# Splitting the first chunk's features one block earlier, and a decode ring of two buffers behind it

## The chip, the cores and the metric

The kernel runs on one core of one Trainium2 chip. The metric is the time of one execution in device microseconds (us): 709.61 us before, the median of 3 runs (709.57 to 710.03). Lower is better.

## The reference

Three layers follow each other. First comes attention over a sliding window of 64 positions (4 sequences of 576 tokens, 8 heads of 64). Its 2304 tokens of width 512 then pass a dense feed-forward layer, and a mixture of 8 experts picks one expert per token.

```python
def _moe_ref(x, w_in, w_out):
    h = x @ w_in                      # 2304x512 @ 512x2048
    g = np.where(h >= 1, h, np.where(h <= -1, 0.0, (h + 1) ** 2 / 4))
    return g @ w_out                  # 2304x2048 @ 2048x512
def _moe2_ref(x, modality_id, w_gate, modality_bias, w1, w2):
    logits = x @ w_gate + modality_bias[modality_id]
    e_idx = np.argmax(logits, axis=1)
    ...
        h = np.maximum(x[mask] @ w1[e], 0.0)
        out[mask] = gate_w[mask, None] * (h @ w2[e])
```

The weights `w_in` and `w_out` arrive as 64-bit floating-point words, which the kernel turns into 32-bit floats itself.

## The kernel before

The dense layer works through 6 chunks of 384 tokens (`NC = 6`, `CT = 384`). Each chunk runs over 16 blocks of 128 features (`NF = 16`). For block f, `l1(c, f)` multiplies the chunk's tokens with w_in tile (0, f), the ScalarE (ACT) and VectorE (DVE) apply the activation (`relu` on ACT, `act2` on DVE), and two steps later `l2(c, f)` (`LAG = 2`) multiplies the result with w_out tile (1, f). A weight tile is called (kind, f), with kind 0 for w_in and 1 for w_out.

**Whole and split.** A 32-bit product can be made in two ways. Whole: the tile is used as it is; each matmul then appears in the trace as two instructions (L508 for `l1`, L575 for `l2`). Split: the operand is rounded to a high part by ACT (`split_hi`, L330, for weights; `gsplit_hi`, L561, for activations), DVE subtracts it to get a low part (`split_lo`, L335; `gsplit_lo`, L566), and three matmuls high-high, high-low, low-high stand for each product (L529 and L581). In chunk 0 the blocks below `FS` are whole and those from `FS` on are split. The chunk's tokens are split by `x0_hi` and `x0_lo` in the steps FS-3 and FS-2. Every later chunk uses split tiles alone, so all 32 weight tiles must be split by the time that chunk 1 needs them.

**Decode.** The 64-bit words come in 16 pairs of tiles. Pair p is loaded by SyncE (SP) with two DMAs of 512 KB (`dec_load`, L273), read by ACT (`dec_abs`, L284, from pair 11 on also L286), then clamped and merged by DVE (`dec_clamp`, L293; `dec_merge`, whose last line is L310 or L312). The words lie in a ring of three buffers, pair p in buffer p % 3. So the load of pair p + 3 can go when pair p is merged. Buffers 0 and 1 are halves of the tile `dec`; buffer 2 lies in the tags T30 and T31. `turn[f]` lists the pairs decoded in step f: pairs 7 and 8 in step 6, pair 9 in step 7, pair 10 in step 8, and then one in each step to pair 15 in step 13. `dec_abs` of a pair runs in the step ahead.

**Where split tiles live.** A split tile needs a buffer (a tag T0 to T31). `free` is the list of tags that can be had, first in, first out. A decoded pair gives its tag back when both its tiles have been split. `soon` lists the splits made during chunk 0. The rest, `later`, is split during chunk 1, at the start of each step: two tiles each, but one in steps 5 and 7.

**Feature blocks 10 to 15 of chunk 1** have their `l1` run ahead, in chunk 0's steps 10 to 15 (`FJ = 10`). Their activations wait in three tiles `kept` (tags T25, T28, T29, two blocks in each) and are split in chunk 1's steps 1 to 6. Their tags join `free` in steps 2, 4 and 6:

```python
        if c == 1 and 1 <= f <= NF - FJ:
            gsplit(1, FJ + f - 1)
            if f % 2 == 0:
                free.append(f"T{NF + (9, 12, 13)[f // 2 - 1]}")
```

The split activations `gh` and `gl` have two buffers each.

**Order.** In chunk 0 (`step0`) the order on TensorE (PE), DVE, ACT and GpSimd (POOL) is the order in which the code writes it. From chunk 1 on, a planner orders DVE, ACT and POOL; PE is again in written order from step 3 of chunk 1. There a step is: `gsplit`, attention for chunk 2, `split`, `l1(1, f)`, `l2(1, 8 + f)` for f below 8, `l2(1, f - 2)`. SP is in written order throughout.

Of the kernel before, what the change touches and what calls it, by code (L numbers as in the profile page):

```python
# [21 lines left out]
DM = H * D  # L22
KD = DM // P
FF = 2048
NF = FF // P
# [49 lines left out]
def moe_kernel(ctx, tc, qT, kT, v, w_in, w_out, mod, wg, wgT, mbias, w1, w2, cst, tri, empty, out, spec):  # L75
# [17 lines left out]
    def tile_of(shape, name, dt=F32, tag=None, bufs=1):  # L93
        pool = sb if (tag or name) in WIDE else sm
        return pool.tile(shape, dt, name=name, tag=tag or name, bufs=bufs)
# [48 lines left out]
    def load_v(i):  # L144
        n, w0 = window(i) if i else (P, 0)
        if i == 1:
            vs[i] = vs[0]
            return
        vs[i] = lend(2 + i // 2, i % 2) if i < BPC else tile_of([P, DM], f"v{i}", tag="v", bufs=2)
        SP.dma_start(vs[i][:n], v[w0 : w0 + n, :])  # L150
# [58 lines left out]

    PRE = 3  # L210
    LAG = 2
    FS, FJ = 9, 10
    TWICE = (6,)

    def part(kind, f, lo):
# [24 lines left out]
    NPR = len(pairs)  # L240
# [1 line left out]
    for f in range(FS, NF - 1):  # L242
        soon.setdefault(f + 1, []).append((1, f))
    soon[NF - 1].append((1, NF - 1))
    for f, kf in ((14, (0, 0)), (14, (0, 1)), (15, (0, 2)), (15, (1, 0))):
        soon[f].append(kf)
    turn, p = [], 1
    for f in range(NF + 1):
# [2 lines left out]
    later = [kf for kfs in pairs for kf in kfs if kf not in sum(soon.values(), [])]  # L251
    lone_kf = later[-1]
    dts = {}

    late = {}

    def raw(p, u):
        if p % 3 == 2:
            if (p, u) not in late:
                late[p, u] = tile_of([P, 2 * DM], f"dec{p}_{u}", I32, tag=f"T{2 * NF - 2 + u}")  # L260
            return late[p, u]
        o = (p % 3 * 2 + u) * 2 * DM
        return dec[:, o : o + 2 * DM]

    def words(p, u):
# [3 lines left out]
    def dec_load(p, us=(0, 1)):  # L269
        if p < NPR:  # L270
            for u in us:
                kind, f = pairs[p][u]
                SP.dma_start(raw(p, u), (w_out if kind else w_in)[f].bitcast(I32))  # L273

    def three(p):
        return p >= turn[FS][0]

    def dec_abs(p, us=(0, 1)):
        if p < NPR:
# [8 lines left out]
    def dec_clamp(p, us=(0, 1)):  # L288
        if p < NPR:
            t = dts[p]  # L290
            for u in us:
                tf = t[u].bitcast(F32)
                V.tensor_scalar(tf, tf, d0 if three(p) else c0, d1 if three(p) else c1, op0=ALU.max, op1=ALU.min)  # L293
            for u in us if not three(p) else ():
                V.tensor_scalar(t[u], t[u], 5, 2, op0=ALU.logical_shift_left, op1=ALU.logical_shift_right)
# [37 lines left out]
    def split_lo():  # L333
        kf, t, tag, w = halves.pop(0)
        V.tensor_tensor(t[:, WB:], w, t[:, :WB].bitcast(F32), op=ALU.subtract)  # L335
        parts[kf] = (t, tag)
        if kf != lone_kf:
            p = pair_of[kf]
            left[p] -= 1
            if not left[p]:  # L340
                free.append(f"T{p}")
# [94 lines left out]
    def att_sum(i):  # L436
        sm = at[i][1]
        V.tensor_scalar_add(sm, sm, 1e-9)
        V.reciprocal(sm, sm)  # L439
# [24 lines left out]
    def att_pv(i):  # L464
        o = 0
        if i < BPC:
            xo = ps.tile([P, KD, BLK], F32, name=f"xo{i}", tag="h", bufs=2)
        elif i < PAIRED:
            xo = aux([P, KD, BLK], f"xo{i}")
        else:  # L470
            o = i % GB
            xo = xos[i - 1] if o else aux([P, KD, GT], f"xo{i}")
        ts = at.pop(i)
        vt = vs.pop(i)
        w = window(i)[0]
        for hp in range(KD):
            for a in range(2):
                c = turned(i, a)
                T.matmul(
                    xo[a * D : (a + 1) * D, hp, o * BLK : (o + 1) * BLK],  # L480
                    vt[:w, (2 * hp + a) * D : (2 * hp + a + 1) * D],
                    ts[:w, hp, c * BLK : (c + 1) * BLK],
                    start=True,
                    stop=True,
                )
        xos[i] = xo

    def att_x(i):
        xo = xos.pop(i)
        c, n = divmod(i, BPC)  # L490
        dst = slice(n * BLK, (n + 1) * BLK)
        if i >= PAIRED:
            xos.pop(i + 1)
            dst = slice(n * BLK, n * BLK + GT)
        if c == 0:
            A.copy(whole_x[0][:, :, dst], xo)
            return
        xh, xl = xs[c]
        A.copy(xh[:, :, dst], xo)
        V.tensor_tensor(xl[:, :, dst], xo, xh[:, :, dst].bitcast(F32), op=ALU.subtract)  # L500
# [9 lines left out]
    def l1_tile(t):  # L510
        if t == 0:
            hs[0, 0] = ps.tile([P, CT], F32, tag="h", name="h0_0", bufs=2)
        l1_whole(0, slice(t * P, (t + 1) * P))
# [18 lines left out]
    def relu(c, f):  # L532
        h = hs[c, f]
        u = tile_of([P, CT], f"u{c}_{f}", tag="u", bufs=2)
        A.activation(u, h, AF.Relu, bias=half, scale=0.5)  # L535
        A.activation(u, u, AF.Square)  # L536
        us[c, f] = u

    def act2(c, f):
        u, h = us[c, f], hs.pop((c, f))  # L540
        g = u
        if c == 1 and f >= FJ:
            j, o = divmod(f - FJ, 2)
            if not o:
                kept.append(tile_of([P, 2 * WB], f"kept{j}", tag=f"T{NF + (9, 12, 13)[j]}"))
            g = us[c, f] = kept[j][:, o * CT : (o + 1) * CT]
        if c == 0 and f < FS:
            g = gs[c, f] = tile_of([P, CT], f"g{c}_{f}", tag="gh" if f % 2 else "gl", bufs=2)
        V.scalar_tensor_tensor(g, u, 1.0, h, op0=ALU.min, op1=ALU.max)  # L549
# [8 lines left out]
    def gsplit_hi(c, f, u):  # L558
        gh = tile_of([P, CT], f"gh{c}_{f}", F32R, tag="gh", bufs=2)
        gl = tile_of([P, CT], f"gl{c}_{f}", F32R, tag="gl", bufs=2)  # L560
        A.copy(gh, u)  # L561
        gs[c, f] = (gh, gl)

    def gsplit_lo(c, f, u):
        gh, gl = gs[c, f]
        V.tensor_tensor(gl, u, gh.bitcast(F32), op=ALU.subtract)  # L566
# [483 lines left out]
    dec_abs(1, (1,))  # L1050
    l1_tile(1)
    l1_tile(2)
    dec_load(3)

    S0 = {c: (1, 5, 9) for c in range(NC)}
    S0[1] = (0, 3, 6)
# [49 lines left out]
    def step0(f):  # L1106
        split0 = f - 1 >= FS
        join = f >= FJ
        at_step = {f - st: BPC + k for k, st in enumerate(FIRST)}
        if f == NF - 3:  # L1110
            free.extend(f"T{NF + k}" for k in (14, 15))
        if f >= 1:
            act2(0, f - 1)
            if split0:
                gsplit_hi(0, f - 1, us[0, f - 1])
        if f - 1 >= FJ:
            act2(1, f - 1)
        for kf in soon.get(f, []):
            split_lo()
        if split0:  # L1120
            gsplit_lo(0, f - 1, us[0, f - 1])
        dec_clamp(*turn[f][:1] or [NPR])
        if 3 in at_step:
            att_pv(at_step[3])
        if 1 in at_step:
            att_sum(at_step[1])
        if 3 in at_step:
            att_x(at_step[3])
        dec_merge(*turn[f][:1] or [NPR])
        for p in turn[f][1:]:  # L1130
            dec_clamp(p)
            dec_merge(p)
        l1(0, f)
        relu(0, f)
        if 1 in at_step:
            load_v(at_step[1])
        two = [at_step[0], at_step[0] + 1] if at_step.get(0, 1) % 2 == 0 else []
        if two:
            att_mm(*two)
            for i in two:  # L1140
                att_loads(i)
        for p in turn[f]:
            dec_load(p + 3)
        if 2 in at_step:
            att_tr(at_step[2])
        for p in turn[f + 1][:1]:
            dec_abs(p)
        if 1 in at_step:
            att_scale(at_step[1])
        if f in (FS - 3, FS - 2):  # L1150
            x0_hi(f - FS + 3)
        for i in two:
            att_max(i)
        if 0 in at_step:
            att_exp(at_step[0])
        if f in (FS - 3, FS - 2):
            x0_lo(f - FS + 3)
        if join:
            l1(1, f)
            relu(1, f)  # L1160
        if f >= LAG:
            l2(0, f - LAG)
        for p in turn[f + 1][1:]:
            dec_abs(p)
        for kf in soon.get(f + 1, []):
            split_hi(kf)
        if f == FS - 1:
            token_bias()
        if f == NF - 1:
            free.extend(f"T{NF + k}" for k in (10, 11))  # L1170
            hold_back(gs[0, f - 1][0].bitcast(F32))
            wgb.append(tile_of([P, E, DM], "wgb", tag="dec"))
            SP.dma_start(
                wgb[0].rearrange("p e d -> p (e d)"),
                wgT.rearrange("(o e) d -> o (e d)", o=1).broadcast_to([P, E * DM]),
            )
# [7 lines left out]
    for n in range(len(its) + LAG):  # L1184
        c, f = its[n] if n < len(its) else (NC, n - len(its))
# [4 lines left out]
        if c == 0:  # L1190
            step0(f)
            continue
# [145 lines left out]
```

## Time and profile before

| what | value |
|---|---|
| median of 3 runs | 709.61 us |
| the profiled execution's own time | 710.55 us |
| its span, first to last instruction | 708.7 us |
| PE, DVE, ACT busy | 697.2, 458.9, 383.3 us |
| mean granted clock of TensorE | 0.998 of full |

The profiled execution lasts 1.85 us longer than its span, and 0.94 us longer than the median. A time in a view counts from the first instruction. A matmul that is still draining counts as busy, so a short wait shows best in the starts of the instructions, which the timeline gives; L529 is line 529 of the kernel. In the timeline a row holds start, duration, engine, line, operation, out<-in and how many were joined; brackets give the idle time ahead and what ended it.

### The profile page before, as it was taken

The numbers are of one execution on the slowest core, as the hardware profiler recorded it, in microseconds if no ns is written. First come the engines' busy times: TensorE is split into PE (matmuls) and PEld (weight loads), VectorE is DVE, ScalarE is ACT, GpSimd is POOL, SyncE is SP. The second block draws the span as 40 slices with busy tenths as digits, with TensorE's granted clock in tenths as the row PEclk, the third lists the DMA queues.
The fourth block names the chain that finished last, engine by engine and source line by source line (L and its number), as shares of the span: only waits on it lengthen the run. The fifth ranks groups of instructions, "written<-read, shape, count | busy, mean of one in ns | idle before, by whom it ended". The sixth has DMA issues, their size and how long they took to land. (4 is left out here: it accounts for less than half of the span.)

```text
span 708.7 us, 13085 instructions
## 1 busy us (share of the span) xinstructions
PE 697.2 (98%) x4523; PEld 601.2 (85%) x4523; DVE 458.9 (65%) x1408; ACT 383.3 (54%) x930; POOL 129.2 (18%) x188
## 2 busy tenths in 40 slices
PE   8999999999999999999999999999999999999995
PEld 5655799888888888988888998899989999998984
DVE  5999997897497538862697648867665454534110
ACT  6799998656555536554555445545444553443120
POOL 3000201013001201120111502041037414111101
PEclk9999999999999999999999999999999999999999
DMA  8986614402221103220310015145555655446401
GB/s 304 312 298 238 215 36 172 133 8 63 75 81 48 41 13 98 61 68 16 98 46 31 2 45 179 63 88 185 174 118 165 224 178 178 164 150 207 148 6 48
DMA packets 48525, 84.59 MB, mean 119 GB/s; under 512 B 6928, under 2 KB 20880, under 8 KB 48320
## 3 DMA queue, kind: packets, MB, share of 16 engines
q1 hardware_dynamic: 44064, 73.64, 31.9%
q0 software_dynamic: 4240, 9.79, 4.7%
q8 instruction: 38, 0.62, 0.4%
q14 instruction: 39, 0.32, 0.1%
q10 hardware_dynamic: 144, 0.22, 0.1%
HBM read 74.17 MB, written 9.67 MB: 118 GB/s over the span
## 5 line engine op out<-in xcount | busy, mean ns | idle before, releaser
L529 PE MATMUL h<-xh,w 128*128 128x384 f32 x640 | 179.4, 341 | 0.0
L581 PE MATMUL py<-w,gh 128*128 128x512 f32 x522 | 162.0, 392 | 0.0
L529 PEld LDWEIGHTS h<-xh,w 128*128 128x128 f32 x640 | 117.0, 188 | 4.4 <-issue 1.4
L581 PEld LDWEIGHTS py<-w,gh 128*128 128x128 f32 x522 | 96.6, 188 | 16.0
L529 PE MATMUL h<-xl,w 128*128 128x384 f32 x320 | 107.4, 336 | 0.0
L581 PE MATMUL py<-w,gl 128*128 128x512 f32 x261 | 102.8, 397 | 0.9 <-DVE gl L566 0.9
L912 PE MATMUL hp<-zh,e 128*128 128x384 f32 x384 | 101.5, 337 | 0.0
L927 PE MATMUL yo<-e,hm 128*128 128x512 f32 x324 | 93.5, 395 | 0.0
L535 ACT ACTIVATE u<-h,half 128x384 f32<-128x384 f32 x96 | 55.4, 577 | 66.9 <-PE h L529 59.9
L838 DVE TENSOR_TENSOR e<-wr,e 128x512 fp32r<-128x512 f32 x96 | 64.0, 689 | 35.9 <-ACT e L837 33.9
L635 DVE CUSTOM_DVE_ANT_0 prod<-y,wgb 128x512 f32<-128x512 f32 x120 | 85.5, 713 | 1.4
L549 DVE SCALAR_TENSOR_TENSOR u<-u,h 128x384 f32<-128x384 f32 x81 | 44.6, 551 | 61.8 <-ACT u L536 61.6
L561 ACT CAST gh<-u 128x384 fp32r<-128x384 f32 x81 | 41.5, 512 | 64.3 <-DVE u L549 34.4
L912 PEld LDWEIGHTS hp<-zh,e 128*128 128x128 f32 x384 | 69.7, 188 | 1.2 <-DVE hm L915 0.3
L927 PEld LDWEIGHTS yo<-e,hm 128*128 128x128 f32 x324 | 59.6, 188 | 12.0 <-issue 0.6
L449 POOL TENSOR_TENSOR s<-s,sm 128x512 f32<-128x512 f32 (+1 forms) x24 | 27.5, 1149 | 214.7 <-DVE sm L439 71.8
L837 ACT CAST e<-wr 128x512 fp32r<-128x512 f32 x96 | 56.7, 616 | 16.6 <-DMA wr<-in_w 16.3
L912 PE MATMUL hp<-zl,e 128*128 128x384 f32 x192 | 64.3, 335 | 0.0
L529 PEld LDWEIGHTS h<-xl,w 128*128 128x128 f32 x320 | 60.1, 188 | 1.9
L566 DVE TENSOR_TENSOR gl<-u,gh 128x384 fp32r<-128x384 f32 x81 | 45.9, 567 | 24.4 <-ACT gh L561 23.5
L581 PEld LDWEIGHTS py<-w,gl 128*128 128x128 f32 x261 | 48.9, 188 | 11.9 <-DVE gl L566 1.5
L914 ACT ACTIVATE hm<-hp 128x384 fp32r<-128x384 f32 x48 | 23.6, 491 | 55.0 <-PE hp L912 54.9
(235 smaller groups left out, 1026.3 us busy)
## 6 DMA issues: line engine op xcount, KB each, us to landing
wr<-in_w SPq DMA_DIRECT2D x96, 256.0 KB, 3.1
dec<-in_w_in SPq DMA_DIRECT2D x16, 512.0 KB, 5.8
dec<-in_w_out SPq DMA_DIRECT2D x16, 512.0 KB, 4.2
v<-in_v SPq DMA_DIRECT2D x27, 256.0 KB, 3.2
k<-in_kT SPq DMA_DIRECT2D x15, 384.0 KB, 4.2
yd<-y SPq DMA_DIRECT2D x18, 256.0 KB, 2.4
q<-in_qT SPq DMA_DIRECT2D x32, 128.0 KB, 2.9
m<-in_w SPq DMA_DIRECT2D x16, 256.0 KB, 4.9
```

The costliest lines, as they stand in the source:

```text
L449: G.tensor_tensor(s, s, bc(sm, 2, window(i)[0]), op=ALU.mult)
L529: T.matmul(h, wi(f, a)[:, k, :], b, start=n == 0, stop=n == 3 * KD - 1)
L535: A.activation(u, h, AF.Relu, bias=half, scale=0.5)
L549: V.scalar_tensor_tensor(g, u, 1.0, h, op0=ALU.min, op1=ALU.max)
L561: A.copy(gh, u)
L566: V.tensor_tensor(gl, u, gh.bitcast(F32), op=ALU.subtract)
L581: T.matmul(ys[c][t], a[:, sl], wo(f, b), start=f == first and n == 0, stop=f == last and n == 2)
L635: V.tensor_tensor_reduce(prod, yt[t], wgb[0][:, e, :], 1.0, 0.0, ALU.mult, ALU.add, lg[:, t, e : e + 1])
L837: A.copy(wpart(i, p, 0), t)
L838: V.tensor_tensor(wpart(i, p, 1), t, wpart(i, p, 0).bitcast(F32), op=ALU.subtract)
L912: T.matmul(hp, w1s(i, f, k, a), b[:, k, :], start=n == 0, stop=n == 3 * KD - 1)
L927: T.matmul(yo, a[f][:, sl], w2s(i, f, b), start=n == 0, stop=n == 3 * NF2 - 1)
```

## The change

Chunk 0 uses split operands from block 8 on (`FS` 9 to 8), so the tiles (0, 8) and (1, 8) and the activation of block 8 are split in chunk 0, and the tokens are split one step earlier, in steps 5 and 6. Tiles (0, 2) and (1, 0) are no longer split at the end of chunk 0 and move to the front of `later`. The ring of three holds to pair 8 (`LAST3`); from pair 9 on there are two buffers, the halves of `dec`, so pair p + 2 is loaded when pair p is merged. T30 and T31 join `free` in step 7, not in step 13. Which pairs take the three-instruction form (`three`) stays as it was, from pair 11. The list `later` keeps 14 tiles:

- before: (0,3) (1,1) (1,2) (0,4) (1,3) (0,5) (1,4) (0,6) (1,5) (0,7) (1,6) (0,8) (1,7) (1,8)
- after: (0,2) (1,0) (0,3) (1,1) (1,2) (0,4) (1,3) (0,5) (1,4) (0,6) (1,5) (0,7) (1,6) (1,7)

```diff
-    FS, FJ = 9, 10
+    FS, FJ = 8, 10
...
-    for f, kf in ((14, (0, 0)), (14, (0, 1)), (15, (0, 2)), (15, (1, 0))):
+    for f, kf in ((14, (0, 0)), (14, (0, 1))):
         soon[f].append(kf)
...
+    LAST3 = turn[TWICE[0]][-1]
+    ring = [p % 3 if p <= LAST3 else (p - LAST3 - 1) % 2 for p in range(NPR)]
+    after = {}
+    for p in range(3, NPR):
+        after.setdefault(max(n for n in range(p) if ring[n] == ring[p]), []).append(p)
...
-        if p % 3 == 2:
+        if ring[p] == 2:
...
-        o = (p % 3 * 2 + u) * 2 * DM
+        o = (ring[p] * 2 + u) * 2 * DM
...
-        return p >= turn[FS][0]
+        return p >= turn[FS + 1][0]
...
-    dec_load(3)
+    for n in after[0]:
+        dec_load(n)
...
-        if f == NF - 3:
+        if f == TWICE[0] + 1:
             free.extend(f"T{NF + k}" for k in (14, 15))
...
         for p in turn[f]:
-            dec_load(p + 3)
+            for n in after.get(p, []):
+                dec_load(n)
```

## Rows read from the trace of the kernel before

**Rows 1.** The page's part 1: busy us, share of the span, instructions.

```profile
PE 697.2 (98%) x4523; PEld 601.2 (85%) x4523; DVE 458.9 (65%) x1408; ACT 383.3 (54%) x930; POOL 129.2 (18%) x188
```

**Rows 2.** Waits of PE, 40 to 709 us: us in total, times, longest.

```profile
PE py L581 <- DVE gl L566: 0.9, 1, 0.9
```

**Rows 3.** Timeline of PE in chunk 0: step 8 to the start of step 10, and step 11's l2.

```profile
67.98 2.85 PE L508 MATMUL h<-x,raw 128*128 128x384 f32 x8
70.66 0.60 PE L456 MATMUL pt<-cs,wides 128*128 128x128 f32 x4
71.10 2.74 PE L575 MATMUL py<-raw,g 128*128 128x512 f32 x6
73.77 0.69 PE L479 MATMUL xo<-ts,v 128*64 128x64 f32 x16
74.39 0.45 PE L529 MATMUL h<-x0h,w 128*128 128x384 f32 x1
...
76.58 2.74 PE L575 MATMUL py<-raw,g 128*128 128x512 f32 x6
...
90.06 0.63 PE L581 MATMUL py<-w,gh 128*128 128x512 f32 x2
...
92.14 0.33 PE L529 MATMUL h<-x0h,w 128*128 128x384 f32 x1
```

**Rows 4.** Busy us by engine in two stretches of chunk 0 (length, then PE, PEld, DVE, ACT, POOL, clock, DMA).

```profile
60.00:80.00 20.00, 20.00 (x110) 11.95 (x109) 19.97 (x43) 18.27 (x43) 4.79 (x2) 1.00 0.63 224
80.00:100.00 20.00, 20.00 (x103) 17.78 (x102) 18.79 (x36) 19.30 (x37) 0.00 (x0) 1.00 0.31 106
```

**Rows 5.** Timeline of DVE: start and last merge of step 7, start of step 8.

```profile
65.07 0.56 DVE L549 SCALAR_TENSOR_TENSOR g<-u,h 128x384 f32<-128x384 f32 x1
...
69.30 0.69 DVE L312 SCALAR_TENSOR_TENSOR raw<-dec,dt 128x512 int32<-128x512 int32 x1
69.90 0.95 DVE L370 TENSOR_TENSOR x0l<-x,x0h 128x768 fp32r<-128x768 f32 x1
70.76 0.55 DVE L549 SCALAR_TENSOR_TENSOR g<-u,h 128x384 f32<-128x384 f32 x1
```

**Rows 6.** DMA issues, 69 to 71 us: pair 12's two loads (KB each, us to landing).

```profile
dec<-in_w_out SPq DMA_DIRECT2D x1, 512.0 KB, 3.5
dec<-in_w_in SPq DMA_DIRECT2D x1, 512.0 KB, 4.2
```

**Rows 7.** Timeline of ACT, step 8: first read of pair 11, split of (0, 10).

```profile
72.37 0.69 ACT L284 ACTIVATE dt<-dec 128x512 f32<-128x512 f32 x1
...
74.83 0.65 ACT L330 CAST w<-raw 128x512 fp32r<-128x512 f32 x1
```

**Rows 8.** Timeline of PE in chunk 1: end of step 6, l1 of block 7.

```profile
165.69 0.39 PE L581 MATMUL py<-w,gl 128*128 128x512 f32 x1
165.92 0.33 PE L529 MATMUL h<-xh,w 128*128 128x384 f32 x1
...
166.27 0.52 PE L529 MATMUL h<-xh,w 128*128 128x384 f32 x2
```

**Rows 9.** Timeline of ACT there: split of block 15's kept activation, and of tile (0, 8).

```profile
165.89 0.51 ACT L561 CAST gh<-kept 128x384 fp32r<-128x384 f32 x1 [1.22 <-PE py L581]
168.43 0.62 ACT L330 CAST w<-raw 128x512 fp32r<-128x512 f32 x1 [2.02 <-DVE gl L566]
```

**Rows 10.** Timeline of DVE there.

```profile
167.84 0.55 DVE L566 TENSOR_TENSOR gl<-kept,gh 128x384 fp32r<-128x384 f32 x1
...
169.08 0.69 DVE L335 TENSOR_TENSOR w<-raw,w 128x512 fp32r<-128x512 f32 x1
```

**Rows 11.** PE by windows around the last matmul: length, busy, granted clock, DMA.

```profile
701.00:702.00 1.00, 0.13 (x1) 1.00 0.06 16
...
705.00:706.00 1.00, 0.00 (x0) 0.92 0.03 8
706.00:707.00 1.00, 0.00 (x0) 0.50 0.00 0
```

## The prediction

> **What bounds the kernel now.** I read the page's busy shares first: PE is busy 98% of the span, DVE 65%, ACT 54% [rows 1]. That alone proves little, so the second view is the waits of PE. From 40 us to the end it lists one, of 0.9 us [rows 2]. Third is the timeline of PE in the stretch that the change touches: in chunk 0's step 8 each group of matmuls starts where the one ahead ends its share, without a gap [rows 3]. So PE sets the end almost everywhere: PE time taken out there comes off the end, and PE time lost there is added. The fourth view, busy time by windows, shows what is next: in 60 to 80 us DVE is busy 19.97 of 20 us and ACT 18.27, in 80 to 100 us 18.79 and 19.30 [rows 4]. In chunk 0 three engines are nearly full, and work moved between them must be followed step by step.
>
> **What the change takes from PE.** Block 8 changes from whole to split. Its `l1` in whole form runs from 67.98 to 70.66, 2.68 us; in split form (block 9) from 74.39 to 76.58, 2.19 us [rows 3]. That is 0.49 us less. Its `l2` in whole form runs from 71.10 to 73.77, 2.67 us; in split form from 90.06 to 92.14, 2.08 us [rows 3]: 0.59 less. Part of the first of each form is drain of the group ahead, so I take 0.5 for each: PE gains 1.0 us, with bounds 0.9 and 1.1. Nothing on PE is added: tile (0, 8) was split anyway, in chunk 1.
>
> **What it adds to DVE and ACT in chunk 0.** In step 7 DVE gets the low part of (0, 8), priced at 0.69 as another such subtraction [rows 10], 0.60 from start to start. In step 9 it gets the low part of (1, 8), the same, and that of block 8's activation (0.55 [rows 10]). ACT gets two weight rounds of 0.62 and one of an activation, 0.51 [rows 9]. The tokens' split is only one step earlier: 0.86 us on DVE from 69.90 to 70.76 [rows 5], which makes DVE up to 0.86 later at the start of step 7 and even again at its end. I cost all this at nothing, since PE need not wait for it, and check that at the tightest place. Step 7 starts on DVE at 65.07 [rows 5], then at 65.93; behind the 0.47 of `act2` the low part of (0, 8) ends at 67.1. PE starts `l1` of block 8 at 67.98 [rows 3]: 0.9 us to spare. If that cover is gone, it costs the excess, at most the 0.6 us of the subtraction. Between 0 and 0.5 I take 0, as the spare time is larger than the terms' error.
>
> **The ring of two.** Pair 11 is loaded after the merge of pair 9, not of pair 8, and so on to pair 15: five pairs, ten DMAs, each one step later. Before, the merge of pair 9 ends at 69.99 [rows 5]; with 0.86 and 0.60 added it ends at about 71.45. The two words' tiles then go out at 70.85 and 71.5. Loads at that time landed after 3.5 and 4.2 us [rows 6], so they are there at 74.4 and 75.7. ACT wants to read pair 11 at 72.37 [rows 7]. It took from 72.37 to 74.83 for both tiles [rows 7], 1.2 us each, so now it is done at 76.9, 2.1 us late. Queued behind it on ACT are the rounding of (0, 10) and (1, 8), block 8's activation and block 9's `relu`; DVE waits for the first of these. The high part of (0, 10) is then ready at 77.5 and the low part at 78.2. PE reaches `l1` of block 10 at 76.58 plus 2.6 [rows 3], minus the 0.5 gained: 78.7, and needs the low part with its third matmul, 0.35 us later. So 0.8 us are left. I made the same sum for steps 10 to 13: ACT stays 2 to 2.6 us late, because its windows are nearly full [rows 4], PE gets a further 0.5 us ahead, and 0.6 to 1.1 us are left each time; from step 13 on no pair is left to read and ACT recovers. So the ring costs nothing on PE, between 0 and about 2 us should the loads land 2 us later than those of rows 6. I take 0.1. On SP nothing waits behind these loads but loads of the same ring.
>
> **Tags and order in chunk 1.** T30 and T31 come free earlier, which no split waits for, and two splits less at the end of chunk 0 free 2 x 0.62 us of ACT where PE does not wait for it. Both cost nothing. But the list `later` is shifted by two: (0, 7) is now the twelfth tile, where (0, 8) was, and falls in step 6 of chunk 1. Following `free` through the code, exactly one tag is in the list there, T29, which the third `kept` tile gives back in that same step. The twelfth split therefore waits for the split of block 15's kept activation. The trace shows this chain for (0, 8). PE's last matmuls of step 6 (`l2` of block 4) end; only then ACT has a `gh` buffer and rounds the kept activation, at 165.89, released by PE [rows 9]; DVE's low part starts at 167.84 and ends at 168.39 [rows 10]; ACT then rounds the weight tile at 168.43, released by that very instruction, to 169.05 [rows 9]; DVE's low part runs from 169.08 to 169.77 [rows 10]. Before, that tile was needed by `l1` of block 8, a whole step on. Now it is needed by `l1` of block 7, which PE begins at 165.92, right behind the matmuls that start the chain [rows 8]. PE is in written order, so everything behind it waits too, first the `l2` of blocks 15 and 5. Its first matmul can start at 169.1, and its third, which started at 166.27 [rows 8] and reads the low part, at 169.8: a stall of 3.5 us. If DVE did the chain without other work between, its four instructions (0.51, 0.55, 0.62, 0.69 [rows 9, 10]) would end at 168.3, and the stall would be 2.1 us. These are the bounds. I take 3.4: what lies between on DVE is the routing of chunk 0 and block 5's activation, which the change does not touch. No later place can give the stall back, because PE shows no wait after it [rows 2].
>
> **The sum.** -1.0 (block 8 on PE) + 0.1 (chunk 0) + 3.4 (block 7 in chunk 1) = +2.5 us. On the profiled execution: span 708.7 to 711.2, time 710.55 to 713.05. That execution is 0.94 above the median, so on the median 709.61 becomes 712.1, 0.35% slower. A kernel of this kind can be told from no change by about 0.2%, here 1.4 us.
>
> **The rivals.**
>
> *The chain is shorter or the buffer order turns.* If the planner gives the kept activation the `gh` buffer that block 14 leaves, some 2.1 us earlier (one split `l2` of 2.08 us [rows 3]), and keeps its other work behind it, the stall falls to 0 to 1.4 us: 708.6 to 710.0. For it: the planner orders DVE and ACT anew. Against it: in the trace the kept one takes the second buffer [rows 9].
>
> *The ring starves ACT.* The spare 0.6 to 1.1 us are gone when two loads in a row land 2 us later than rows 6 have it. PE then waits up to 2 us more in steps 10 to 13, on top of the sum: 712.5 to 714.5. Against it: in that stretch the only loads are the ring's.
>
> *The clock falls.* If a stall of 3.5 us made TensorE's clock drop to 1.2 GHz, the next step, two split `l2` and one split `l1`, 2 x 2.08 + 2.19 = 6.35 us at 2.4 GHz [rows 3], would take twice that: about 718. Against it: after the last matmul, at 701.13, the granted clock is still 1.00 to 705 and reaches 0.50 only from 706 on [rows 11]. The Trainium skill (TensorE: Matmul & The Clock Gate, "HAM oscillation — how this bites in real kernels") says that a matmul stream broken by waits is throttled again and pays for warming up; no row here shows that within a stream.
>
> *Faster.* The gain of 1.0 stands, the chain comes early enough for block 7, and the one wait of 0.9 us [rows 2] goes too, as DVE's work moves: 709.61 - 1.9 = 707.7. It decides when tile (0, 7) is whole and split by 165.9 minus 1.0. For that T29 would have to come free 3 us earlier, before its reader has a buffer.
>
> **How the numbers follow.** The stall as summed, 710.7 to 712.7: 0.62. Shorter chain: 0.20. Starved ring: 0.12. Clock: 0.02. Faster: 0.04. The forecast is the first, 712.1. From 708.6 to 714.0 all but about 0.09 lies inside: the faster case, the clock and the end of the starved ring. Slower by over 1.4 us: 0.58 of the first case, the ring and the clock, 0.71 rounded to 0.70. Within it: the rest of the first and the shorter chain, 0.24. Faster by more: 0.06 with the errors of the gain.
>
> **What would show it.** Right, if PE's timeline has a gap of 2 to 3.5 us at `l1` of block 7 in chunk 1, with the waits naming DVE's low part of a weight; if the first chunk ends on PE some 1 us earlier; and if ACT in steps 8 to 12 waits for DMA, and PE there does not. Wrong, if block 7 starts without a gap (then the tag or the buffer went another way), or if PE has gaps in steps 8 to 13 (then the ring is what matters).

## The result, and the profile after

The changed kernel takes 714.15 us (median of 6 runs, 712.85 to 715.49) against 709.98 us for the kernel before on the same chip (709.57 to 710.22). The ratio is 1.0065, with a 95% interval of 1.0055 to 1.0076: slower by 4 to 5 us (the two medians alone are 4.2 us apart). The forecast was 712.1 us with a range of 708.6 to 714.0. The direction and the place were right; the loss was larger, and one of its parts had been put down as nearly excluded.

The waits of PE in the changed kernel, from 40 us to the end (us in total, times, longest), are three where [rows 2] had one:

```profile
PE h L534 <- ACT w L335: 3.0, 1, 3.0
PE py L586 <- DVE gl L571: 0.8, 1, 0.8
PE xo L484 <- ACT ts L466: 0.4, 1, 0.4
```

The second is the old wait. The first is new and stands where it was expected. The timeline of PE in the changed kernel, end of chunk 1's step 6 and `l1` of block 7 (L534 is the former L529), answers to [rows 8]:

```profile
164.66 0.39 PE L586 MATMUL py<-w,gl 128*128 128x512 f32 x1
168.01 0.54 PE L534 MATMUL h<-xh,w 128*128 128x384 f32 x1 [2.97 <-ACT w L335]
168.35 0.52 PE L534 MATMUL h<-xl,w 128*128 128x384 f32 x1
168.74 1.01 PE L534 MATMUL h<-xh,w 128*128 128x384 f32 x2
...
171.72 0.34 PE L534 MATMUL h<-xh,w 128*128 128x384 f32 x1
171.90 0.62 PE L586 MATMUL py<-w,gh 128*128 128x512 f32 x2
```

In the kernel before, the first matmul of `l1` follows that last one after 0.23 us [rows 8]; here it would start at 164.89. It starts at 168.01, waiting for the rounding of the weight tile. The chain behind it, from the timelines of ACT and DVE of the changed kernel, is the one of [rows 9, 10], link by link and 1.1 us earlier:

```profile
164.85 0.51 ACT L566 CAST gh<-kept 128x384 fp32r<-128x384 f32 x1 [1.21 <-PE py L586]
167.34 0.62 ACT L335 CAST w<-raw 128x512 fp32r<-128x512 f32 x1 [1.98 <-DVE gl L571]
```

```profile
166.77 0.54 DVE L571 TENSOR_TENSOR gl<-kept,gh 128x384 fp32r<-128x384 f32 x1
...
167.99 0.69 DVE L340 TENSOR_TENSOR w<-raw,w 128x512 fp32r<-128x512 f32 x1
```

But the block takes longer still once it runs: from 168.01 to the `l2` at 171.90 are 3.9 us, where the block's twelve matmuls need 2.1. Some 0.5 us of the 1.8 belong to the chain: the third matmul, at 168.74, reads the low part, which DVE finishes at 168.68. The windows of PE in the changed kernel (length, busy, granted clock, DMA) show the rest:

```profile
167.00:168.00 1.00, 0.00 (x0) 1.00 0.00 0
168.00:169.00 1.00, 0.99 (x3) 0.61 0.00 0
169.00:170.00 1.00, 1.00 (x4) 0.50 0.00 0
170.00:171.00 1.00, 1.00 (x5) 0.50 0.03 1
171.00:172.00 1.00, 1.00 (x6) 0.69 0.03 1
172.00:173.00 1.00, 1.00 (x6) 1.00 0.02 1
```

While PE waits, the granted clock stands at full; just after it has work again, the clock falls to 0.50, 1.2 GHz, for about 3.4 us (the four windows below 1.00 lack 0.39, 0.50, 0.50 and 0.31 us of full speed, 1.70 in all, which at half speed takes 3.4). No row of the kernel before had shown that within its work.

The first chunk went as laid out, with one small wait. Timeline of PE, the kernel before, from step 7 of chunk 0 to the first step of chunk 1 (two more rows of it):

```profile
61.57 2.85 PE L508 MATMUL h<-x,raw 128*128 128x384 f32 x8
...
117.30 0.89 PE L399 MATMUL sc<-k,q 64*64 64x128 f32 x24
```

and the same of the changed kernel:

```profile
60.94 2.85 PE L513 MATMUL h<-x,raw 128*128 128x384 f32 x8
...
67.18 0.69 PE L484 MATMUL xo<-ts,v 128*64 128x64 f32 x16 [0.38 <-ACT ts L466]
67.79 0.45 PE L534 MATMUL h<-x0h,w 128*128 128x384 f32 x1
...
116.15 1.10 PE L404 MATMUL sc<-k,q 64*64 64x128 f32 x32
```

From step 7 to chunk 1 it is 55.73 us before and 55.21 after: 0.5 us gained. The 0.38 us wait lies inside; without it the gain is 0.9. (Step 7 itself begins 0.6 us earlier, ahead of anything the change touches, so the end of chunk 0 alone would overstate the gain.) The waits of ACT in 55 to 120 us of the changed kernel show the ring at work:

```profile
ACT dt L289 <- DMA dec<-in_w_out: 3.0, 2, 2.2
...
ACT dt L289 <- DMA dec<-in_w_in: 0.6, 1, 0.6
```

ACT waits 3.6 us for loads that it never waited for before, and PE, as summed, does not wait for any of it (its 0.38 us wait stays when the ring of three is kept, experiment 4).

### The profile page after: what moved, and what is told of

Same layout as the page of the kernel before. It is cut to its first block, busy times and chain, and to the rows that moved or that the text cites. A ratio compares the mean times of both kernels' runs of the same rounds, so it can differ in the third digit from the quotient of the medians.

```text
span 712.2 us, 13102 instructions
## 1 busy us (share of the span) xinstructions
PE 697.5 (98%) x4530; PEld 603.7 (85%) x4530; DVE 459.8 (65%) x1409; ACT 384.6 (54%) x931; POOL 127.1 (18%) x188
## 5 line engine op out<-in xcount | busy, mean ns | idle before, releaser
L534 PE MATMUL h<-xh,w 128*128 128x384 f32 x640 | 180.8, 343 | 3.0 <-ACT w L335 3.0
L586 PE MATMUL py<-w,gh 128*128 128x512 f32 x528 | 163.9, 392 | 0.0
L534 PEld LDWEIGHTS h<-xh,w 128*128 128x128 f32 x640 | 117.8, 189 | 8.1 <-ACT w L335 3.4
L534 PE MATMUL h<-xl,w 128*128 128x384 f32 x320 | 108.0, 338 | 0.0
L566 ACT CAST gh<-u 128x384 fp32r<-128x384 f32 x82 | 42.1, 513 | 65.5 <-DVE u L554 29.9
L571 DVE TENSOR_TENSOR gl<-u,gh 128x384 fp32r<-128x384 f32 x82 | 46.4, 566 | 25.8 <-ACT gh L566 23.4
L534 PEld LDWEIGHTS h<-xl,w 128*128 128x128 f32 x320 | 60.6, 189 | 1.9
```

The lines of the kernel that those rows point to most:

```text
L534: T.matmul(h, wi(f, a)[:, k, :], b, start=n == 0, stop=n == 3 * KD - 1)
L586: T.matmul(ys[c][t], a[:, sl], wo(f, b), start=f == first and n == 0, stop=f == last and n == 2)
```

## The experiments

Two theories stood at the start. A: the chain of the tag T29 in front of `l1` of block 7, and the low clock that follows its wait, are the whole loss. B: the ring of two, or the fuller first chunk, costs by itself. Each ratio is to the kernel before, run on the same chip; that kernel's median was 711.01 us beside experiments 1 to 4, 710.94 beside 5, 6, 7 and 10, and 710.12 beside 8 and 9.

**1. Another tile takes the waiting place.**

```diff
     lone_kf = later[-1]
+    i, j = later.index((1, 5)), later.index((0, 7))
+    later[i], later[j] = later[j], later[i]
```

> The changed kernel with tiles (0,7) and (1,5) exchanged in the list of later splits, so that the split that waits for T29 is that of (1,5), which the matmuls need two groups of matmuls later. Theory A (the tag chain and the clock drop behind it are the whole loss): no wait of PE at l1 of block 7, granted clock 1.00 there, and the time is that of before less the 1.15 us that PE gained in chunk 0: 708.5 to 709.2, 5 us under the changed kernel. Theory B (the ring of two and the earlier splits cost by themselves): 711 to 714, with PE still behind.

Measured: 710.43 us, ratio 0.9991 (0.9982 to 1.0000). No wait of PE at block 7, clock 1.00 there: its `l1` runs from 164.96 to 167.07 without a gap.

```profile
164.96 0.33 PE L536 MATMUL h<-xh,w 128*128 128x384 f32 x1
...
167.07 0.63 PE L588 MATMUL py<-w,gh 128*128 128x512 f32 x2
```

All of the loss is gone with two lines of order. What is left of the gain, 0.6 us, is nearer to the 0.5 us of the trace than to the 1.15 us that was expected. A holds, and B is out for anything above some tenths.

**2. The same chain put into the kernel before.**

```diff
+    i, j = later.index((0, 7)), later.index((0, 8))
+    later[i], later[j] = later[j], later[i]
+    later.remove((0, 7))
+    later.insert(later.index((1, 6)), (0, 7))
...
-            split(1 if f in (5, 7) else 2)
+            split({5: 0}.get(f, 2))
```

> The kernel before, with nothing changed but the order of its later splits, so that (0,7) is the split that waits for T29 (one step later than before: no split in step 5 of chunk 1, two in step 7). Theory A: the same wait of PE of about 3 us at l1 of block 7 and the same fall of the clock behind it, 713.5 to 716. Theory B: within 0.5 us of before, since ring, first split block and chunk 0 are those of before.

Measured: 716.07 us, ratio 1.0066 (1.0050 to 1.0081). Here (0, 7) is the first split of step 6, and so the one that finds T29 alone in the list. Without any of the change's ring, block or chunk 0, the order of the later splits alone makes the same loss, 5.1 us as in experiment 5. The waits and the windows of PE in this kernel:

```profile
PE h L533 <- ACT w L334: 3.0, 1, 3.0
PE py L585 <- DVE gl L570: 0.9, 1, 0.9
```

```profile
168.00:169.00 1.00, 0.40 (x2) 1.00 0.00 0
169.00:170.00 1.00, 0.89 (x6) 0.97 0.00 0
170.00:171.00 1.00, 1.00 (x5) 0.50 0.02 1
```

**3. Work for PE in the gap.**

```diff
+        if (c, f) == (1, 7):
+            filler = aux([P, CT], "filler")
+            for _ in range(14):
+                T.matmul(filler, wi(6, 0)[:, 0, :], xs[1][0][:, 0, :], start=True, stop=True)
         if n < len(its):
             l1(c, f)
```

> The changed kernel with 14 extra matmuls (128x384, the result is not used) between the l2 of block 4 and the l1 of block 7 in chunk 1, about 2.4 us of the 3 us in which PE waits. The chain of the split stays as it is. Theory A with the clock as a loss of its own: PE resumes at the same moment, the clock stays at 1.00, and the time is about 1.7 us under the changed kernel's profiled run, 712 to 713 with little spread between runs. If the clock has no part in it: 714 as the changed kernel, with its spread.

Measured: 714.01 us, ratio 1.0043 (1.0027 to 1.0058). That is 3.0 us over the kernel before beside it; the expected 712 to 713 was missed, but it was reckoned from first runs that stand 1.0 us lower. PE comes to block 7 no earlier, but the clock stays. Timeline and windows of PE in this kernel:

```profile
165.17 2.62 PE L1227 MATMUL filler<-xh,w 128*128 128x384 f32 x14
168.36 0.45 PE L534 MATMUL h<-xh,w 128*128 128x384 f32 x1 [0.57 <-ACT w L335]
...
170.95 0.63 PE L586 MATMUL py<-w,gh 128*128 128x512 f32 x2
```

```profile
168.00:169.00 1.00, 0.62 (x2) 1.00 0.00 0
169.00:170.00 1.00, 0.91 (x5) 1.00 0.00 0
```

This splits the loss in two. From the end of step 6 to the `l2` it is 170.95 - 165.17 = 5.78 us, 3.67 more than the 2.11 that block 7 takes unhindered: the chain. In the changed kernel it is 171.90 - 164.89 = 7.01, 4.90 more: another 1.23 us for the clock. The low stretch can lie later and then slows the matmuls behind block 7 too. Counted to the first attention matmul of step 8 (operand `pt`), it is 9.91 us here, 11.10 in the changed kernel, 11.40 in its repeat (experiment 5) and 11.43 in experiment 2: a fall costs 1.2 to 1.5 us.

**4. The ring of three kept, with the exchange of the first experiment.**

```diff
-    ring = [p % 3 if p <= LAST3 else (p - LAST3 - 1) % 2 for p in range(NPR)]
+    ring = [p % 3 for p in range(NPR)]
...
-        if f == TWICE[0] + 1:
+        if f == NF - 3:
```

> The first of these kernels (exchanged tiles) with the ring of three buffers kept for all pairs and T30 and T31 given back in step 13 as before. Prediction's step (the ring costs PE nothing, 0.1 us): the same time as the exchanged kernel within 0.3 us, and the waits of ACT for the loads in steps 8 to 10 (3.6 us in the changed kernel) are gone. Theory B: 1 us or more under the exchanged kernel.

Measured: 710.38 us, ratio 0.9991 (0.9982 to 1.0000), that of experiment 1 to the last digit. ACT's waits for the loads are gone, and nothing is gained by it. The ring of two costs nothing that these runs can show; the interval is 0.6 us wide to either side.

**5. The changed kernel once more,** unchanged.

> The changed kernel itself once more, beside the others on one chip. Theory A (wait of PE plus a low clock behind it): 4 to 5 us over before, more spread than before, and its executions ordered by the granted clock, the slower the lower. If the spread has another cause, clock and time are not in one order.

Measured: 716.08 us, ratio 1.0075 (1.0062 to 1.0089). Its five executions, with their mean granted clock over the whole span: 715.46 and 715.72 us at 0.994; 716.08, 716.36 and 717.38 at 0.992. They spread over 1.9 us and stand in the order of the clock. The loss is 5.1 us, a little above the expected 4 to 5. The mean clock has to be read with care, as it also counts the fall after the last matmul, which costs no time: the profile of experiment 9 has a mean of 0.996 with no low window at block 7. The profiled execution here, at 0.994, has one low stretch at block 7 (169 to 173 us) and that fall at the end. An estimate from these figures: the low stretch lacks 1.7 us of full speed and the fall at the end 2.4, while a mean of 0.992 over 714 us lacks at least 5.4. So the three slower executions would have had further low time, which no profile here shows.

**6. Less work in the gap:** 6 extra matmuls in place of experiment 3's 14, the rest of the edit alike.

> The changed kernel with 6 extra matmuls (result not used) in place of 14 ahead of l1 of block 7: PE waits about 2.0 us without a matmul, where the changed kernel has 3.0 and the one with 14 has 0.6. If the clock falls whatever the gap, the low stretch stays and the time is that of the changed kernel; if it falls only because of the long gap, the clock stays at 1.00 and the time is that with 14 extra matmuls, some 1.2 us less.

Measured: 714.84 us, ratio 1.0061 (1.0046 to 1.0076), not clearly apart from either. PE waits 1.9 us in the profiled execution and the clock stays at 1.00. Its waits and a window of PE:

```profile
PE h L534 <- ACT w L335: 1.9, 1, 1.9
```

```profile
169.00:170.00 1.00, 0.89 (x6) 1.00 0.00 0
```

Three executions of 714.28 to 715.11 us have a clock of 0.997 or 0.998; the fourth, 716.70 us, has 0.995. So neither expectation held as stated: by these times and clocks, the fall comes in some executions and not in others, though only the first of the four has a profile. This one is inconclusive on how long a gap may be.

**7. The kept activation split first, so that it takes the earlier buffer.**

```diff
             act2(*its[n - 1])
+            if (c, f) == (1, 6):
+                gsplit(1, FJ + f - 1)
             gsplit(*its[n - 1])
...
         if c == 1 and 1 <= f <= NF - FJ:
-            gsplit(1, FJ + f - 1)
+            if f < NF - FJ:
+                gsplit(1, FJ + f - 1)
```

> The changed kernel with one order turned round in chunk 1's step 6: block 15's kept activation is split ahead of block 5's, so that it takes the gh buffer which the l2 of block 14 gives back, 2.1 us earlier. Theory A (the chain starts at that buffer): the wait of PE at l1 of block 7 shrinks from 3.0 us to about 1 us, the clock stays at 1.00, and the time falls by 2.5 to 3.5 us against the changed kernel. Rival: DVE's other work sets the start of the chain; then the wait shrinks by less than 0.7 us.

Measured: 713.43 us, ratio 1.0034 (1.0024 to 1.0045). The wait fell to 1.8 us, not to 1. ACT rounds the kept activation 1.7 us earlier, counted from the end of step 6. ACT and DVE of this kernel:

```profile
163.41 0.50 ACT L566 CAST gh<-kept 128x384 fp32r<-128x384 f32 x1
166.40 0.62 ACT L335 CAST w<-raw 128x512 fp32r<-128x512 f32 x1 [2.50 <-DVE gl L571]
```

```profile
163.52 0.14 DVE L705 COPY alloc<-inc 128x1 f32<-128x1 f32 x1
...
163.78 1.00 DVE L680 TENSOR_TENSOR nf<-ns,nblk 128x8 f32<-128x8 f32 x1
...
165.82 0.54 DVE L571 TENSOR_TENSOR gl<-kept,gh 128x384 fp32r<-128x384 f32 x1
```

The high part is ready at 163.9, yet the low part starts only at 165.82: DVE works through the routing of chunk 0 and block 5's activation, in the order that the planner fixed. Both theories of that expectation were half right: the buffer starts the chain, and DVE's queue sets its length. In the profiled execution, 714.45 us, the clock fell behind this shorter gap too (waits and a window of PE):

```profile
PE h L534 <- ACT w L335: 1.8, 1, 1.8
```

```profile
169.00:170.00 1.00, 1.00 (x5) 0.56 0.00 0
```

Over the eight executions the clock runs from 0.998 (712.69 us) to 0.994 (714.98 us).

**8. The routing moved out of the way, alone.**

```diff
-        for _ in range(2 if c == 1 and f >= 4 else 1):
+        for _ in range({4: 2, 5: 0, 6: 0}.get(f, 3 if f > 6 else 1) if c == 1 else 1):
```

> The changed kernel with the routing moved alone. The chain starts at the same release (end of the l2 of block 4), but runs back to back: the lower bound of the prediction. First matmul of l1 of block 7 waits about 1.6 us, the low part costs another 0.5: 2.1 us in all against 3.7 in the changed kernel, so 1.6 us less, and 2.8 to 3 us less in the executions in which the clock does not fall.

Measured: 712.34 us, ratio 1.0032 (1.0021 to 1.0044). The first matmul waits 1.6 us, as expected: the chain's four instructions start at 165.28, 165.82, 166.41 and 167.06, with no routing between them. The loss is 2.2 us. The executions are not quite in the order of the clock (712.74 us at 0.995, 711.50 at 0.996). The clock fell in the profiled execution, 713.84 us; the windows of PE:

```profile
168.00:169.00 1.00, 1.00 (x5) 0.67 0.00 0
169.00:170.00 1.00, 1.00 (x5) 0.50 0.00 0
```

**9. Both, experiments 7 and 8 together.**

> The changed kernel with both delays in the chain taken out: block 15's kept activation split ahead of block 5's (its buffer comes 2.1 us earlier), and chunk 0's routing moved from chunk 1's steps 5 and 6 to steps 7 to 9, so that DVE has no small work between the chain's instructions. Theory A with DVE as the second part of the chain: the wait of PE at l1 of block 7 is 0.5 us or less, the clock stays, and the time is that of the changed kernel less 4 to 5 us, at or under before. Rival (the chain's length is set by something not seen): a wait of 1.5 us or more stays.

Measured: 710.58 us, ratio 1.0005 (0.9996 to 1.0015). Block 7 loses 0.7 us: its `l1` starts at 165.30, its `l2` at 167.87, and a gapless one would have gone from 165.04 to 167.15. The clock stays at 1.00 there. So the chain is made of its four instructions, the buffer at its head and DVE's other work; what is left to explain is at most these 0.7 us. About 0.5 of them stand in the trace: DVE's low part of the kept activation (L571, 163.57) took 1.03 us, where it takes 0.54 in the changed kernel, while a GpSimd multiplication was under way from 163.14 to 164.18.

**10. A version that beats both:** the exchange of experiment 1, and the kept activation split first in all six steps, which is the order in which the `l2` matmuls take them.

```diff
             act2(*its[n - 1])
+            if c == 1 and 1 <= f <= NF - FJ:
+                gsplit(1, FJ + f - 1)
             gsplit(*its[n - 1])
...
         if c == 1 and 1 <= f <= NF - FJ:
-            gsplit(1, FJ + f - 1)
```

> The exchange of (0,7) and (1,5), and the kept activation split first in all six steps, as the l2 matmuls want it. Theory A: no wait of PE at block 7, and the old wait of 0.8 us at l2 of block 12 gets shorter or goes: 0.2 to 0.9 us under the kernel with the exchange alone, 1.0 to 1.9 us under before. Rival: the wait at block 12 comes from DVE's load in that stretch and stays: the time of the kernel with the exchange alone.

Measured: 709.80 us, ratio 0.9983 (0.9974 to 0.9992), 1.1 us under the kernel before, where experiment 1 was 0.6 us under. It is the only version here whose interval lies wholly under the kernel before; that of experiment 1 overlaps with it, so the step from one to the other is not settled by the times. The waits of PE in this kernel, from 40 us on:

```profile
PE yo L934 <- ACT hm L921: 0.6, 1, 0.6
PE py L588 <- DVE gl L573: 0.5, 1, 0.5
PE xo L486 <- ACT ts L468: 0.4, 1, 0.4
```

The old wait at `l2` of block 12 went from 0.8 to 0.5 us, 0.3 us less. Counted from chunk 0's step 7 to the end of step 6, PE takes 103.14 us against 103.94 in experiment 1; the other 0.5 lie between 128 and 135 us, where the planner still orders PE. The one on L934 lies in the expert layer, far from the edit.

## Why the prediction was right and where it failed

**Right: PE sets the end.** Every wait put into PE's stream came out in the time, and experiment 1 gave it back when the wait was gone.

**Right: the gain in chunk 0,** 1.0 us summed, 0.9 measured without the 0.4 us wait. That wait is a small miss of the step "I cost all this at nothing": the place that was checked, the low part of (0, 8) ahead of block 8, held, but ACT's copy `ts` (L466) slipped behind the new rounding and held up the attention matmuls by 0.38 us.

**Right: the ring.** ACT late by about 2 us, PE not held up; experiment 4 shows it as a difference of nothing.

**Right: the tag.** T29 is the only tag in the list, the twelfth split waits for it, and the twelfth split is (0, 7). Summed 3.4 us, with bounds 2.1 and 3.5; measured 3.67 in experiment 3, a little outside. (From its own rows the lower bound is 168.3 - 166.27 = 2.0; experiment 8, where the four run back to back, has its third matmul at 167.81, 2.1 us late.)

**Wrong: the clock.** The step that failed is the rival "The clock falls" and its "Against it: after the last matmul, at 701.13, the granted clock is still 1.00 to 705". It took one fall, at the end of the kernel, for what happens in any gap, and gave the rival a chance of 0.02. (The prediction's chances of being slower by over 1.4 us add to 0.72, not 0.71.) That fall was not a bound even for the end of the kernel: in experiment 9 the last matmul ends at 700.98 and the clock begins to fall between 703.0 and 703.5, after little over 2 us and not over 4. And the step left out that the clock can fall when PE is already back at work. The clock did fall, in the changed kernel after a gap of 3.0 us and in the profiles of experiments 8 and 7 after gaps of 1.6 and 1.8. The rival's price was wrong as well, but the other way: it charged half speed for a whole step, 6.35 us more, where the low stretch lasted 3.4 us and cost block 7 1.23 us, and 1.5 us in two other profiles. With what was measured, the sum is -0.9 + 0.4 + 3.7 + 1.2 = +4.4 us on 709.98: 714.4, beside the 714.15 that was found. Without the clock it would be 713.2, inside the range. The repeat lost 5.1, which this sum does not reach. The Trainium skill (TensorE: Matmul & The Clock Gate, "HAM oscillation — how this bites in real kernels") says that a matmul stream broken by waits is throttled again. These traces agree in kind, with a granted clock of 0.50 from 169 to 171 us in the changed kernel, though the waits in the Trainium skill's example are longer than the 1.6 to 3.0 us here.

**What stays open** is why the clock falls in one execution and, by the times and mean clocks, not in the next of the same kernel (experiments 6 and 7), and where the slowest executions of the changed kernel lose their further time (experiment 5). A gap of 1.9 us was followed by full clock in one profile and one of 1.8 us by half clock in another, so the length of the gap does not settle it.

## What to carry to other kernels

When a list of work is shifted, follow what the shift does to the last free buffer: here the first split of step 6 waits for it in every version, and all depends on which tile that is. A wait just ahead of the bounding engine's next instruction costs the whole chain behind it, including the unrelated work that a planner has put between its links. And a gap in a matmul stream should be priced twice, for itself and for a slower clock after it, with a range for the second, as by the times here it comes in some executions only.

## What the runs showed of the hardware

- The clock fell after PE had resumed, not during the gap: in the changed kernel it reads 1.00 in 167 to 168 us, with no matmul, and 0.50 two windows later with PE busy. The same order stands in the profiles of experiments 2, 5, 7 and 8, and in all five the low stretch is 3.4 us long, worked out from the windows as above. The clock also fell with as little as 1.6 us of wait (experiment 8), and stayed at 1.00 with 1.9 us (experiment 6).
- After the last matmul, which costs no time, the clock fell too, but not after a fixed time: it begins to fall between 705 and 706 us in the kernel before, where that matmul ends at 701.13, and between 703.0 and 703.5 in experiment 9 (mean 0.71 there), where it ends at 700.98.
- A DVE instruction over 8 elements took 1.00 us in experiment 7 (L680, 163.78); its neighbours of up to that size take 0.14 to 0.17 (L705 among them). In the changed kernel the same instruction runs from 163.52 to 164.52, and a GpSimd multiplication over 512 elements was under way there, from 163.39 to 164.50. Both timelines of the changed kernel:

```profile
163.39 1.11 POOL L454 TENSOR_TENSOR s<-s,sm 128x512 f32<-128x512 f32 x1 [1.04 <-DVE ns L679]
```

```profile
163.52 1.00 DVE L680 TENSOR_TENSOR nf<-ns,nblk 128x8 f32<-128x8 f32 x1
```

The small instruction ends with the other engine's. Larger ones end a little later than it: in experiment 8 a low part over 384 elements (L571) takes 1.03 us and ends at 164.87, the GpSimd multiplication at 164.45; in the kernel before, the one in front of the old wait (L566, 144.44) takes 1.38 us in place of 0.55 and ends at 145.82, the multiplications at 145.41. So part of the old wait may come from there. That the two engines wait for each other was seen in these places, not tested.
